# An HGRN2 attention and mixer kernel: the scheduler's load order instead of a written one, fewer idle products, and stores in two halves of columns

## The chip, the cores and the metric

The kernel runs on one core of a Trainium2 chip. The metric is the device time of one execution in microseconds (us). TensorE (PE) multiplies matrices, and its weight loads are recorded apart (PEld). VectorE (DVE), ScalarE (ACT) and GpSimd (POOL) work on elements. SyncE (SP) issues nearly all transfers between HBM and on-chip memory; its queue is in order, so an entry that has to wait holds up all entries behind it.

## The reference

```python
batch, n_heads, seq, head_dim = 4, 8, 768, 48
f = 1.0 / (1.0 + np.exp(-f_logit))
for t in range(S):                                   # a gated outer-product state
    state = f[:, :, t, :, None] * state + np.einsum('bhd,bhe->bhde', k[:, :, t], v[:, :, t])
    y[:, :, t] = np.einsum('bhd,bhde->bhe', q[:, :, t], state)

x = y.transpose(0, 2, 1, 3).reshape(B, S, H * D)      # (4, 768, 384)
h = x.transpose(0, 2, 1) @ U @ V                      # low rank over the sequence, rank 32
u = x + h.transpose(0, 2, 1)
out = u + np.maximum(u @ w_ch1, 0.0) @ w_ch2          # 384 -> 1536 -> 384
```

The inputs q, k, v and f_logit are float32. U, V, w_ch1 and w_ch2 are float64 (8 bytes), and the kernel itself turns their words into float32.

## The kernel before

The attention works on units: two heads of one batch. There are 16 units, four (`HP = 4`) for each batch; units 0 to 3 are the first batch. A unit has eleven steps, five in front (gates, keep, keys, read_back, queries) and six in the rear (kept, states, scan, scores, read, inner). The raw f, k and q of a unit lie in one of two buffers, so the loads of unit n+2 have to wait for the transposes of unit n; v lies in one of three. The first batch's attention has no mixer of an earlier batch to run beside it. After it, the mixer of batch 0 runs beside the attention of batch 1, and so on.

A weight comes in two parts: `start` issues its load, `end` turns it into float32 with two ACT, three DVE and one POOL instruction. The list `weights` has 27 entries: U, two of V (`early = 3`), 12 pieces of w_ch1 (w1[0] to w1[11], 128 columns and 384 KB each) and 12 of w_ch2. The first six pieces of w_ch1 (`FIRST = 6`) are loaded into three `zw` buffers that are free at the start; all other weights are loaded into the four `w_raw` buffers (`RAW = 4`).

Everything on PE, DVE and ACT in the part below keeps its written order. `manual_schedule` says for which engines the written order holds; the other engines' instructions are ordered when the program is compiled, by a scheduler that takes the earliest written instruction that is ready in its own model of the time.

```python
    FIRST = 6
    for _ in range(FIRST // 2):
        t = zp.tile([P, NFC // 2, 2 * P], F32, name="zw").rearrange("p i t -> p (i t)")
        spare.extend([t[:, 0 : 2 * WP], t[:, 2 * WP : 4 * WP]])

    held = spare[2][:, 0:1]                   # a column of the place of w1[2]
    nc.gpsimd.memset(held, 0.0)
    # ... cut ...
        def follow(nm):                       # called when a unit's nm has been transposed
            if n + 2 < NU and n + 2 not in (HP, HP + 1):
                load(n + 2, nm)
    # ... cut ...
        def busy(n):
            for _ in range(n):
                nc.tensor.matmul(idle[:, 0:DM], lhsT=ident, rhs=ends[:, 0:DM], start=True, stop=True)

        with tc.manual_schedule(engines={nc.vector.engine, nc.scalar.engine, nc.sync.engine}):
            busy(1)
            for piece in front(0, "gates"):
                piece()
            for n in range(HP):
                pieces = front(n, "keep", "keys") + rear(n - 1, "scan", "scores")
                pieces += [lambda: busy(3)] + rear(n, "kept") + front(n, "read_back", "queries")
                if n + 1 < HP:
                    pieces += front(n + 1, "gates") + rear(n - 1, "read", "inner") + rear(n, "states")
                for piece in pieces:
                    piece()
                if n < 2:
                    load(n + 2, "v")
                if n == 1:
                    for start, _ in weights[: early + 2]:
                        start()
            # ... cut: ends of U, V, w1[0] and the last steps of units 2 and 3 ...
            low_rank_of(done)
            nc.scalar.copy(table, held)       # the load of w1[2] may not overwrite this column earlier
            for i in range(2):
                for start, _ in weights[early + 2 * i + 2 : early + 2 * i + 4]:
                    start()
                load(HP + i, "f", "k", "q", "v")
            for start, _ in weights[early + FIRST : early + FIRST + RAW]:
                start()
            ends_of[early + 1]()
            # ... cut: rest of the low-rank part ...
            loads = ahead_by(FIRST - 2 + RAW, weights[early + 2 :])
```

`ahead_by(n, loads)` makes a list of calls; call i issues the start of entry i + n and then does the end of entry i. These calls stand between the first products of the mixer of batch 0. In those, `ch1(a, j)` (line 258 of the kernel, tile `pz`) multiplies by the pieces w1[2j] and w1[2j + 1], for each of the three pairs a of token blocks.

From batch 1 on, the second product of a pair of token blocks is done with seven products instead of eight, in four steps:

```python
        def store(t, o):
            nc.sync.dma_start(out=out[b, t * P : (t + 1) * P, :], in_=o)
        # ... cut ...
            if step == 0:
                # ... cut ...
                add(o[:, lo], s[:, lo], pm[:, hi], ALU.add)      # left half of block 2a is final
            # ... cut: steps 1 and 2; step 2 stores block 2a + 1 ...
            else:
                pm = products(a, (S[a, 4], w2[:, NI:NFC, hi]))
                add(W["o0"][:, hi], W["s"][:, hi], pm[:, lo], ALU.add)
                store(2 * a, W["o0"])
```

Of the kernel before, what the change touches and what calls it, by code (L numbers as in the profile page):

```python
# [10 lines left out]
F32 = mybir.dt.float32  # L11
U32 = mybir.dt.uint32
U64 = mybir.dt.uint64
# [5 lines left out]
WP = 384  # L19

RAW = 4
# [125 lines left out]
class Mixer:  # L147
# [6 lines left out]
    def __init__(self, tc, b, x, U, V, w1, w2, sums, ident, blocks, out, two, three, zp, ps_big, ps_mm, wide=False,  # L154
                 z_all=None, room=None, pair=0):
        nc = tc.nc
        P = nc.NUM_PARTITIONS
        NCH, DM = x.shape[1], x.shape[2]
# [25 lines left out]
        def add(*args):  # L184

            with tc.high_priority(offset=AHEAD):
                nc.vector.tensor_tensor(*args)  # L187
# [79 lines left out]
                    z[a, c] = zp.tile([P, NI, 2 * P], F32, name="zw" if wide and c == 1 else "z")  # L267
            nc.scalar.activation(z[a, c][:, k : k + 2, :].rearrange("p i t -> p (i t)"), pm, AF.Relu)  # L268

        def store(t, o):  # L270
            nc.sync.dma_start(out=out[b, t * P : (t + 1) * P, :], in_=o)

        po = {}
        NQ = 4
# [41 lines left out]
        W = {}  # L316
        lo, hi = slice(0, HM), slice(HM, DM)

        def seven(a, step):
            x0, x1 = x[:, 2 * a, :], x[:, 2 * a + 1, :]  # L320
            if step == 0:
                pm = products(a, (part(a, 0, 0), w2[:, 0:NI, lo]), (part(a, 0, 1), w2[:, NI:NFC, lo]))
                s = W["s"] = two.tile([P, WP], U32, name="w_y").bitcast(F32)
                o = W["o0"] = three.tile([P, DM], F32, name="o")
                nc.scalar.copy(s[:, hi], pm[:, lo])
                add(s[:, lo], x0[:, lo], pm[:, lo], ALU.add)
                add(o[:, lo], s[:, lo], pm[:, hi], ALU.add)
            elif step == 1:
                pm = products(a, (S[a, 2], sums[2]), (S[a, 3], sums[3]))
                s, o = W["s"], W["o0"]  # L330
                add(s[:, hi], s[:, hi], pm[:, lo], ALU.add)
                add(o[:, hi], s[:, hi], pm[:, hi], ALU.add)
                o1 = W["o1"] = three.tile([P, DM], F32, name="o")
                add(o1.rearrange("p (n d) -> p n d", n=2), x1.rearrange("p (n d) -> p n d", n=2),
                    o[:, hi].unsqueeze(1).broadcast_to((P, 2, HM)), ALU.add)
                add(s[:, hi], s[:, hi], x0[:, hi], ALU.add)
            elif step == 2:
                pm = products(a, (part(a, 1, 1), sums[4]), (S[a, 1], sums[1]))
                add(W["o1"], W["o1"], pm[:, 0:DM], ALU.add)
                store(2 * a + 1, W["o1"])  # L340
                add(W["s"][:, hi], W["s"][:, hi], pm[:, hi], ALU.add)
            else:
                pm = products(a, (S[a, 4], w2[:, NI:NFC, hi]))
                add(W["o0"][:, hi], W["s"][:, hi], pm[:, lo], ALU.add)
                store(2 * a, W["o0"])

        sums_x, values = {}, {}
        FG = NFC // 3
# [124 lines left out]
def factored_path(ctx, tc, q, k, v, f_logit, moe_U, moe_V, moe_w_ch1, moe_w_ch2, out, ok):  # L473
# [56 lines left out]
    def load(n, *names):  # L530

        b, hp = divmod(n, HP)
        for nm in names:
            if nm == "v":
                v_tiles[n] = three.tile([P, NBL, 2, D], F32, name="v_nat")
            for par in range(2):
                head = src[nm][b, 2 * hp + par]
                if nm == "v" and par:

                    for s in range(2):  # L540
                        nc.sync.dma_start(
                            out=v_tiles[n][(1 - s) * C : (2 - s) * C, :, par, :],
                            in_=head.rearrange("(c s p) d -> s p c d", s=2, p=C)[s],
                        )
                    continue
                if nm == "v" or n < TURNED:
                    dst = v_tiles[n] if nm == "v" else nat[n % 2][nm]
                    nc.sync.dma_start(out=dst[:, :, par, 0:D], in_=head.rearrange("(c p) d -> p c d", p=P))  # L548
                    continue
                head = head.rearrange("(c i) d -> i c d", i=NB)  # L550
                for part in range(2):
                    p0 = par * PAD + part * NB
                    n_ch = min(NB, D - part * NB)
                    nc.sync.dma_start(  # L554
                        out=raw[n % 2][nm][p0 : p0 + NB, :].rearrange("p (c d) -> p c d", d=NB)[:, :, 0:n_ch],
                        in_=head[:, :, part * NB : part * NB + n_ch],
                    )
# [55 lines left out]

    spare = []

    FIRST = 6
    for _ in range(FIRST // 2):
        t = zp.tile([P, NFC // 2, 2 * P], F32, name="zw").rearrange("p i t -> p (i t)")
        spare.extend([t[:, 0 : 2 * WP], t[:, 2 * WP : 4 * WP]])


    held = spare[2][:, 0:1]
    nc.gpsimd.memset(held, 0.0)

    def place():
        return spare.pop(0).bitcast(U64)

    weights += [
        take_in(w1[:, :, i * P : (i + 1) * P], w1_rows[:, :, i * P : (i + 1) * P], place if i < FIRST else None)
        for i in range(NFC)  # L630
# [271 lines left out]
    def front(n, *names):  # L902

        if n >= NU:
            return []
        if n not in ahead:
            ahead[n] = dict(zip(("gates", "keep", "keys", "read_back", "queries"), prepare(n)))
        return [ahead[n].pop(nm) for nm in names]

    def rear(n, *names):  # L910

        if not 0 <= n < NU:
            return []
        if n not in here:
            here[n] = dict(zip(("kept", "states", "scan", "scores", "read", "inner"), attend(n)))
        return [here[n].pop(nm) for nm in names if nm in here[n]]
# [43 lines left out]
    with tc.manual_schedule(engines={nc.vector.engine, nc.scalar.engine}):  # L960


        idle = ps_mm.tile([P, 512], F32, name="idle", tag="mm")

        def busy(n):
            for _ in range(n):
                nc.tensor.matmul(idle[:, 0:DM], lhsT=ident, rhs=ends[:, 0:DM], start=True, stop=True)

        with tc.manual_schedule(engines={nc.vector.engine, nc.scalar.engine, nc.sync.engine}):
            busy(1)  # L970
            for piece in front(0, "gates"):
                piece()
            for n in range(HP):
                pieces = front(n, "keep", "keys") + rear(n - 1, "scan", "scores")
                pieces += [lambda: busy(3)] + rear(n, "kept") + front(n, "read_back", "queries")
                if n + 1 < HP:
                    pieces += front(n + 1, "gates") + rear(n - 1, "read", "inner") + rear(n, "states")
                for piece in pieces:
                    piece()
                if n < 2:  # L980
                    load(n + 2, "v")
                if n == 1:


                    for start, _ in weights[: early + 2]:
                        start()


            done, rest = slice(0, 2 * n * D), slice(2 * n * D, DM)
            ends_of = [end for _, end in weights]  # L990
            pieces = rear(n, "states") + rear(n - 1, "read") + rear(n, "scan") + ends_of[:1] + rear(n, "scores")
            pieces += ends_of[1:2] + rear(n - 1, "inner") + rear(n, "read") + ends_of[2 : early + 1]
            for piece in pieces:
                piece()
            m = mixer(0)
            low_rank_of, added_up_of, mix_of = m.some
            low_rank_of(done)

            nc.scalar.copy(table, held)
            for i in range(2):  # L1000
                for start, _ in weights[early + 2 * i + 2 : early + 2 * i + 4]:
                    start()
                load(HP + i, "f", "k", "q", "v")
            for start, _ in weights[early + FIRST : early + FIRST + RAW]:
                start()
            ends_of[early + 1]()
            for piece in rear(HP - 1, "inner"):
                piece()
            added_up_of(done)
            low_rank_of(rest)  # L1010
            mix_of(done)
            added_up_of(rest)
            mix_of(rest)
            loads = ahead_by(FIRST - 2 + RAW, weights[early + 2 :])

        start = m.before[3:5] + m.firsts[0:1] + m.before[5:]

        EARLY = 6
        second = chain(front(HP, "gates", "keep", "keys", "read_back", "queries"), steps(HP, 2 * HP + 1))
        for i, (_, piece) in enumerate(start + m.firsts[1:]):  # L1020
            piece()
            if loads:
                loads.pop(0)()
            if i >= EARLY:
                next(second)()
        for f in loads:
            f()
        n = len(m.seconds) // (NBL // 2)
        todo, after = m.seconds[:-n], m.seconds[-n:]

        attention(second, 12 + 10 * HP - (len(start) + len(m.firsts) - 1 - EARLY), todo)
        m = start_mixer(1, after)
        for f in to_sum:
            f()
# [380 lines left out]
```

## Time and profile before

| what | value |
|---|---|
| time, median of 3 runs | 495.2 us (494.14 to 495.38) |
| span of the profiled execution | 493.6 us |
| PE busy | 473.2 us (96%), 5541 products |
| DVE busy | 355.6 us (72%) |
| ACT busy | 162.9 us (33%) |
| POOL busy | 37.4 us (8%) |
| transfers on the one queue | 33.44 MB, 37.8% of 16 engines' span |
| stores of the output | 24 of 192 KB |

The profile's page gives busy times over the whole span and, in 40 slices of 12.3 us, the tenths in which each engine was busy. PE is busy in nearly all slices, so what matters is where it is not, and where its clock is halved. In the timeline, a group is given with its start, its length, engine, line, operation, tiles and count, and in brackets the idle time of the engine before it with the instruction that ended that idle time. A stretch (of the view of stretches) is a row with one sum of busy time for each engine, the granted clock of PE as a share of full speed, the share of time in which the transfer engines were busy (which can come out above 1 where transfers overlap) and the rate.

### The profile page before, as it was taken

To read this page: it belongs to the slowest core of one execution; us is meant where nothing else is said; L and a number is where in the kernel's file an instruction comes from. 1 tells how busy PE (TensorE), PEld (TensorE's weight loads), DVE (VectorE), ACT (ScalarE), POOL (GpSimd) and SP (SyncE) were. 2 spreads that over 40 slices of the span, in tenths; PEclk is the share of its full clock that TensorE was granted. 3 is DMA by queue.
4 is the path that set the end of the run, shared out by engine and by line. 5 is a ranking of instruction groups with operands and counts; after the bars stand their busy time and mean duration, and the time that the engine had idled before them with its cause. 6 is when DMAs were issued, how large, how long until landed. Compare 5 with 4: busy or idle time off the path is not lost.

```text
span 493.6 us, 12736 instructions
## 1 busy us (share of the span) xinstructions
PE 473.2 (96%) x5541; PEld 403.5 (82%) x5541; DVE 355.6 (72%) x563; ACT 162.9 (33%) x310; POOL 37.4 (8%) x50
## 2 busy tenths in 40 slices
PE   7898969999999999999999999999999999999995
PEld 4676758887666558889889878899979999999995
DVE  5879548777988949567657637888797796958742
ACT  3336345565344304432331313433132221211200
POOL 3002224443100000000000000000000000000000
PEclk9999898999999999999999999999999999999999
DMA  9981997658577714251725300100000000000001
GB/s 145 155 158 47 218 213 182 162 126 153 71 118 126 123 32 62 28 73 25 106 28 85 68 17 17 27 3 19 19 1 0 34 2 16 17 1 33 1 33 38
DMA packets 158679, 34.34 MB, mean 70 GB/s; under 512 B 149206, under 2 KB 157078, under 8 KB 158614
## 3 DMA queue, kind: packets, MB, share of 16 engines
q1 hardware_dynamic: 158614, 33.44, 37.8%
q8 instruction: 45, 0.74, 0.6%
q14 instruction: 20, 0.16, 0.1%
HBM read 28.70 MB, written 4.72 MB: 68 GB/s over the span
## 4 chain that ended last, share of the span: by engine, by line
PE 69%; DVE 13%; SPq 7%; DMA 4%; issue 3%; ACT 2%; POOL 0%; DVEq 0%; ACTq 0%
PE pw L312 25%; PE pz L258 17%; PE pp L410 11%; SPq L548 3%; PE y L886 2%; PE y L868 2%; SPq L554 2%; DVE late L699 2%; PE ds L830 2%; DVE late L717 2%; PE po L283 2%; PE sc L793 2%; DMA late<-in_f_logit_dram 2%; PE pt L665 1%; PE put L246 1%
## 5 line engine op out<-in xcount | busy, mean ns | idle before, releaser
L258 PE MATMUL pz<-uT,w 128*128 128x256 f32 x504 | 118.6, 390 | 4.7 <-ACT z_all L268 3.4
L258 PEld LDWEIGHTS pz<-uT,w 128*128 128x128 f32 x504 | 95.2, 194 | 18.8 <-ACT z_all L268 3.6
L312 PE MATMUL pw<-w,z_all 128*128 128x192 f32 x216 | 37.7, 329 | 0.0
L312 PE MATMUL pw<-zw,w_raw 128*128 128x192 f32 x216 | 37.4, 327 | 0.0
L312 PEld LDWEIGHTS pw<-zw,w_raw 128*128 128x128 f32 x216 | 35.2, 190 | 0.8 <-issue 0.6
L312 PEld LDWEIGHTS pw<-w,z_all 128*128 128x128 f32 x216 | 35.0, 190 | 0.7
L95 POOL TENSOR_TENSOR w<-w_y,w_r 128x384 int32<-128x384 int32 x24 | 31.2, 1301 | 48.2 <-DVE w_y L94 36.3
L699 DVE TENSOR_TENSOR_SCAN late<-fz,late 128x768 f32<-128x768 f32 x16 | 28.1, 1755 | 9.1 <-ACT fz L686 4.4
L268 ACT ACTIVATE z_all<-pz 128x512 f32<-128x512 f32 x33 | 19.6, 595 | 40.9 <-PE pz L258 40.9
L410 PE MATMUL pp<-v_nat,late 128*128 128x128 f32 x224 | 28.8, 275 | 0.0
L92 DVE TENSOR_SCALAR w_y<-w_y 128x384 f32<-128x384 f32 (+3 forms) x27 | 13.6, 504 | 21.0 <-ACT w_y L90 20.7
L717 DVE TENSOR_TENSOR_SCAN late<-fz,other 128x768 f32<-128x768 f32 x16 | 27.9, 1744 | 0.1
L410 PEld LDWEIGHTS pp<-v_nat,late 128*128 128x128 f32 x224 | 27.0, 192 | 0.0
L283 PE MATMUL po<-w,zw 128*128 128x384 f32 x72 | 25.6, 499 | 0.0
L283 PE MATMUL po<-w,z_all 128*128 128x384 f32 x72 | 25.3, 496 | 0.3 <-DVE o L187 0.3
L403 ACT ACTIVATE other<-other 128x512 f32<-128x512 f32 x18 | 11.3, 631 | 39.9 <-DVE other L187 39.9
L856 ACT COPY st<-added 128x576 f32<-128x576 f32 x12 | 14.7, 1223 | 27.5 <-DVE added L851 27.5
L800 DVE TENSOR_TENSOR A<-sc,causal 128x768 f32<-128x768 f32 x16 | 15.1, 947 | 9.9 <-PE sc L793 9.9
L283 PEld LDWEIGHTS po<-w,z_all 128*128 128x128 f32 x72 | 13.1, 190 | 8.7 <-DVE o L187 0.9
L283 PEld LDWEIGHTS po<-w,zw 128*128 128x128 f32 x72 | 12.9, 189 | 8.7 <-issue 1.2
L187 DVE TENSOR_TENSOR w_raw<-z_all 128x768 f32<-128x768 f32 x12 | 11.4, 954 | 10.6 <-ACT z_all L268 9.2
L886 PEld LDWEIGHTS y<-v_nat,A 64*64 64x64 f32 x768 | 13.3, 139 | 6.7 <-ACT seen L875 3.4
(195 smaller groups left out, 833.3 us busy)
## 6 DMA issues: line engine op xcount, KB each, us to landing
w_raw<-in_moe_w_ch_dram SPq DMA_DIRECT2D x18, 384.0 KB, 3.9
out_dram<-o SPq DMA_DIRECT2D x24, 192.0 KB, 1.9
v_nat<-in_v_dram SPq DMA_DIRECT2D x16, 144.0 KB, 2.9
v_nat<-in_v_dram SPq DMA_DIRECT2D x32, 72.0 KB, 3.2
zw<-in_moe_w_ch_dram SPq DMA_DIRECT2D x6, 384.0 KB, 5.0
late<-in_f_logit_dram SPq DMA_DIRECT2D x10, 96.0 KB, 3.3
late<-in_k_dram SPq DMA_DIRECT2D x10, 96.0 KB, 3.0
late<-in_q_dram SPq DMA_DIRECT2D x10, 96.0 KB, 2.7
```

The costliest lines, as they stand in the source:

```text
L95: nc.gpsimd.tensor_tensor(dst.bitcast(I32), shaped(y.bitcast(I32)), shaped(r), ALU.add)
L258: nc.tensor.matmul(pm[:, i * 2 * P : (i + 1) * 2 * P], lhsT=w1[:, m, o : o + P], rhs=uT[a][:, m, :], start=(m == 0), stop=(m == NDC - 1))
L268: nc.scalar.activation(z[a, c][:, k : k + 2, :].rearrange("p i t -> p (i t)"), pm, AF.Relu)
L283: nc.tensor.matmul(pm, lhsT=z[a, i // NI][:, i % NI, s * P : (s + 1) * P], rhs=w2[:, i, :], start=(i == 0), stop=(i == NFC - 1))
L312: nc.tensor.matmul(pm[:, n * HM : (n + 1) * HM], lhsT=lhs[:, i, :], rhs=rhs[:, i, :], start=(i == 0), stop=(i == NI - 1))
L410: nc.tensor.matmul(pm[:, i, r * P : (r + 1) * P], lhsT=room["w"](wn)[:, r * P : (r + 1) * P], rhs=x_node(a, xn), start=((xn, wn) == of[0]) ...
L548: nc.sync.dma_start(out=dst[:, :, par, 0:D], in_=head.rearrange("(c p) d -> p c d", p=P))
L699: nc.vector.tensor_tensor_scan(backwards(X, S - 1, S), backwards(f, S, S), backwards(ends, S - 1, S), 0.0, ALU.mult, ALU.add,)
L717: nc.vector.tensor_tensor_scan(Y, f[:, 0:S], starts, 0.0, ALU.mult, ALU.add)
L800: nc.vector.tensor_tensor(T["A"], sc[:, :, 0 : NBL * C].rearrange("p h (c i) -> p h c i", i=C), causal.unsqueeze(1).unsqueeze(1).broadcast ...
L856: nc.scalar.copy(st, states.rearrange(by_e, c=NCH))
L886: nc.tensor.matmul(o(s, par, c), lhsT=T["A"][part[s ^ par], par, c, :], rhs=vt[part[s ^ par], c, par, :], start=False, stop=True, skip_gro ...
```

## The change

The changed kernel takes SyncE out of the written order, so the scheduler orders the loads of the first part as it does elsewhere. It drops `held` and the ACT copy that kept the load of w1[2] back. The loads of f, k, q and v of units 4 and 5 are written inside the loop, directly after units 2 and 3 have been transposed; w1[2] to w1[5] are written directly after the loop, and the starts of the later weights stand nine entries ahead of the ends. The idle products, which are there to keep PE's clock up, are left out for units 2 and 3. The three `zw` buffers are taken when they are first needed. The stores of block 2a are made in two halves of columns, each as soon as it is final.

```diff
-        def store(t, o):
-            nc.sync.dma_start(out=out[b, t * P : (t + 1) * P, :], in_=o)
+        def store(t, o, cols=slice(0, DM)):
+            nc.sync.dma_start(out=out[b, t * P : (t + 1) * P, cols], in_=o[:, cols])
...
                 add(o[:, lo], s[:, lo], pm[:, hi], ALU.add)
+                store(2 * a, o, lo)
...
-                store(2 * a, W["o0"])
+                store(2 * a, W["o0"], hi)
...
+    def place():
+        if not spare:
+            t = zp.tile([P, NFC // 2, 2 * P], F32, name="zw").rearrange("p i t -> p (i t)").bitcast(U64)
+            spare.extend([t[:, 0:WP], t[:, WP : 2 * WP]])
+        return spare.pop(0)
+
     FIRST = 6
-    for _ in range(FIRST // 2):
-        t = zp.tile([P, NFC // 2, 2 * P], F32, name="zw").rearrange("p i t -> p (i t)")
-        spare.extend([t[:, 0 : 2 * WP], t[:, 2 * WP : 4 * WP]])
-    held = spare[2][:, 0:1]
-    nc.gpsimd.memset(held, 0.0)
-    def place():
-        return spare.pop(0).bitcast(U64)
...
-        with tc.manual_schedule(engines={nc.vector.engine, nc.scalar.engine, nc.sync.engine}):
... (the body moves out of this block by one level) ...
-                pieces += [lambda: busy(3)] + rear(n, "kept") + front(n, "read_back", "queries")
+            pieces += [lambda: busy(3)] * (n < HP - 2) + rear(n, "kept") + front(n, "read_back", "queries")
...
                 for start, _ in weights[: early + 2]:
                     start()
+            elif n > 1:
+                load(n + 2, "f", "k", "q", "v")
+        for start, _ in weights[early + 2 : early + FIRST]:
+            start()
+        loads = ahead_by(early + FIRST, weights)
...
-            nc.scalar.copy(table, held)
-            for i in range(2):
-                for start, _ in weights[early + 2 * i + 2 : early + 2 * i + 4]:
-                    start()
-                load(HP + i, "f", "k", "q", "v")
-            for start, _ in weights[early + FIRST : early + FIRST + RAW]:
-                start()
-            ends_of[early + 1]()
+        loads[early + 1]()
...
-            loads = ahead_by(FIRST - 2 + RAW, weights[early + 2 :])
+        loads = loads[early + 2 :]
```

More of the change, by code (lines that the diff above doesn't have):

```diff
@@ L967, in busy @@
                 nc.tensor.matmul(idle[:, 0:DM], lhsT=ident, rhs=ends[:, 0:DM], start=True, stop=True)
-        with tc.manual_schedule(engines={nc.vector.engine, nc.scalar.engine, nc.sync.engine}):
[L970 to L974, printed above, removed]
-                pieces += [lambda: busy(3)] + rear(n, "kept") + front(n, "read_back", "queries")
[L976 to L985, printed above, removed]
-                        start()
[L989 to L992, printed above, removed]
@@ L993, in factored_path @@
+        busy(1)
+        for piece in front(0, "gates"):
+            piece()
+        for n in range(HP):
+            pieces = front(n, "keep", "keys") + rear(n - 1, "scan", "scores")
+            pieces += [lambda: busy(3)] * (n < HP - 2) + rear(n, "kept") + front(n, "read_back", "queries")
+            if n + 1 < HP:
+                pieces += front(n + 1, "gates") + rear(n - 1, "read", "inner") + rear(n, "states")
             for piece in pieces:
                 piece()
-            m = mixer(0)
@@ L996, in factored_path @@
-            low_rank_of, added_up_of, mix_of = m.some
-            low_rank_of(done)
-            nc.scalar.copy(table, held)
-            for i in range(2):
-                for start, _ in weights[early + 2 * i + 2 : early + 2 * i + 4]:
-                    start()
-                load(HP + i, "f", "k", "q", "v")
-            for start, _ in weights[early + FIRST : early + FIRST + RAW]:
-                start()
-            ends_of[early + 1]()
-            for piece in rear(HP - 1, "inner"):
-                piece()
@@ L1009, in factored_path @@
[L1009 to L1013, printed above, removed]
-            loads = ahead_by(FIRST - 2 + RAW, weights[early + 2 :])
+            if n < 2:
+                load(n + 2, "v")
+            if n == 1:
+                for start, _ in weights[: early + 2]:
+                    start()
+            elif n > 1:
+                load(n + 2, "f", "k", "q", "v")
+        for start, _ in weights[early + 2 : early + FIRST]:
+            start()
@@ new lines, in factored_path @@
+        loads = ahead_by(early + FIRST, weights)
+        done, rest = slice(0, 2 * n * D), slice(2 * n * D, DM)
+        pieces = rear(n, "states") + rear(n - 1, "read") + rear(n, "scan") + loads[:1] + rear(n, "scores")
+        pieces += loads[1:2] + rear(n - 1, "inner") + rear(n, "read") + loads[2 : early + 1]
+        for piece in pieces:
+            piece()
+        m = mixer(0)
+        low_rank_of, added_up_of, mix_of = m.some
+        low_rank_of(done)
+        loads[early + 1]()
+        for piece in rear(HP - 1, "inner"):
+            piece()
@@ L1016, in factored_path @@
+        added_up_of(done)
+        low_rank_of(rest)
+        mix_of(done)
+        added_up_of(rest)
+        mix_of(rest)
+        loads = loads[early + 2 :]
         start = m.before[3:5] + m.firsts[0:1] + m.before[5:]
```

## The prediction

> **What bounds the kernel now.** I read the busy totals first, then stretches of the first 80 us, then PE's timeline with what it waited for, then SP's queue. The totals and slices of the page:
>
> ```profile
> PE 473.2 (96%) x5541; PEld 403.5 (82%) x5541; DVE 355.6 (72%) x563; ACT 162.9 (33%) x310; POOL 37.4 (8%) x50
> DMA  9981997658577714251725300100000000000001
> ```
>
> PE is the bound over most of the span: only 493.6 - 473.2 = 20.4 us of it are idle. So a gain must come from that idle time, from time at half clock, or from products that needn't be there. The transfers are near full for three slices (to 37 us), stand nearly empty in the fourth (37 to 49 us), and are full again. That hole is made by the kernel. The stretches around it:
>
> ```profile
> 26.00:28.00 2.00, 2.00 (x55) 1.50 (x54) 1.54 (x2) 0.11 (x1) 0.00 (x0) 1.00 1.03 189
> 40.00:42.00 2.00, 1.87 (x100) 1.74 (x92) 1.57 (x2) 0.95 (x3) 0.00 (x0) 1.00 0.01 4
> 44.00:46.00 2.00, 1.40 (x31) 0.71 (x22) 1.86 (x7) 0.94 (x5) 0.79 (x2) 1.00 0.00 0
> 50.00:52.00 2.00, 1.31 (x18) 0.77 (x14) 2.00 (x3) 0.24 (x1) 1.00 (x1) 1.00 1.20 307
> 70.00:72.00 2.00, 0.00 (x0) 0.00 (x0) 0.36 (x1) 0.95 (x3) 0.00 (x0) 1.00 1.09 372
> 74.00:76.00 2.00, 2.00 (x6) 1.55 (x6) 1.93 (x4) 1.74 (x4) 1.04 (x2) 0.50 0.89 232
> ```
>
> The first pair of numbers after the sum is PE's busy time and count, the last three are clock, transfer share and GB/s. From 40 to 46 us nothing is loaded; from 70 to 72 us PE does nothing at all while weights pour in at 372 GB/s; from 74 to 76 us PE runs at half clock. PE's timeline names the wait:
>
> ```profile
> 63.11 5.45 PE L258 MATMUL pz<-uT,w 128*128 128x256 f32 x24 [1.32 <-ACT uT L247]
> 68.39 0.82 PE L665 MATMUL pt<-ident,late 128*128 128x128 f32 x6
> 72.58 7.13 PE L258 MATMUL pz<-uT,w 128*128 128x256 f32 x24 [3.37 <-ACT z_all L268]
> 80.20 5.35 PE L258 MATMUL pz<-uT,w 128*128 128x256 f32 x24
> ```
>
> The engine named, ACT, is itself waiting: the waits list 6.6 us in one piece for its operation on a `w_raw` weight, ended by that weight's transfer (71.05 us). The chain that ended last says the same: SP's issues of unit 4 and 5 from 52.3 us without a break to 66.5 us, then the w1[6] transfer of 3.98 us, then two ACT operations, then the products. And SP's queue shows why the issues are so late:
>
> ```profile
> SPq L81 <- ACT table L999: 13.0, 1, 13.0
> ```
>
> SP stood 13.0 us (34.2 to 47.2 us) before the load of w1[2], waiting for the ACT copy that the kernel put in front of it. Everything behind it waited too.
>
> **What the skill says.** The Trainium skill, "TensorE: Matmul & The Clock Gate", section "Part 1: The HAM clock gate": PE's clock is half when it has been idle for a window of about 3.4 us, and whole again after as long a busy window. The trace agrees in kind: 0.51 at 24 to 26 us and 0.50 at 54 to 56 and 74 to 76 us, each after a gap or a sparse stretch, and 24 products took 7.13 us instead of 5.35 us. This is what the idle products are for. The Trainium skill, "DMA: Bandwidth & Descriptors", section "Why small descriptors are slow (HBM only)": short pieces cost a fixed part each. The trace agrees: unit loads (192 bytes a piece) moved at about 163 GB/s here, w_ch1 pieces at 307 to 372 GB/s. The skill has no page on the scheduler's order, on which much of this rests.
>
> **The change part by part.**
>
> *Idle products of units 2 and 3.* Each group of six takes 2.13 us of the chain (27.28 and 36.09 us). In unit 2 removing it hardly helps: DVE runs without a gap from 26.46 to 34.5 us and is the bound there. In unit 3, DVE waits 0.76 us for the k transposes (35.27 us), which come earlier if PE is 2.1 us ahead; then 0.33 us before the state scan at 41.39 us goes too. I take 1.1 us of the 4.3 us. More does not come, since the remaining DVE chain is solid.
>
> *No hold, loads of units 4 and 5 and w1[2] to w1[5] early.* In the present order SP starts units 2 and 3 without waiting and reaches U at 31.25 us. If the scheduler keeps this written order, unit 4 (1.18 MB, 7.2 us at 163 GB/s) starts at about 35 us, where f, k and q buffers have been free since 20, 25 and 30 us and v since 34 us. Unit 5 follows; its last v load needs the end of unit 2's inner products (47.4 us now, about 46 us then), so SP may stand there briefly. w1[2] to w1[5] (4 x 393 KB at 330 GB/s: 4.8 us) then land by about 50 to 55 us and w1[6] to w1[9] by about 60 us. Now w1[4] is there at 61.4 us (ACT waits 2.2 us for it) and w1[6] at 71.05 us. PE asks for w1[2] near 61 us, for w1[4] near 66 us and for w1[6] near 72 us. So no product should wait for a weight:
>
> - idle before the pz at 72.58 us: 3.37 us;
> - half clock after it: 7.13 - 5.35 = 1.8 us;
> - idle before the pz at 63.11 us (ACT's copy of uT stands behind its wait for w1[4]): 1.3 us.
>
> Sum 6.5 us. The half clock at 54 to 57 us (12 products in 3.68 us against 2.76 us) comes from the sparse low-rank part before it and stays.
>
> *Does it reach the end?* From 72.6 us PE is 100% busy to 120 us, and in 120:150 and 150:176 it is busy 29.1 of 30 and 25.8 of 26 us while DVE is busy 26.4 and 23.9 us. There DVE nearly bounds, but its work is tied to PE's order and should move along. Behind 176 us PE has few gaps. I count nearly all as kept, less something for loads landing differently.
>
> *Half stores.* Nine blocks get a second SP issue of about 0.35 us, beside other work. Only the last one counts: 488.63 us (DVE's last add) to the end at 493.6 us is 5.0 us. The median landing of a 192 KB store is 1.9 us; half of it saves perhaps 0.3 us, because most of a landing is not data.
>
> Sum: 1.1 + 6.5 + 0.3 = 7.9 us, giving 487.3 us.
>
> **Rivals.**
>
> *The scheduler puts weights ahead of the first units.* U, V and w1[0] to w1[5] need no wait, so wherever its model sees SP free while unit 2 or 3 waits for a buffer, they go first. Those 2.7 MB, at 330 GB/s down to the 213 GB/s of the sixth slice of the page, cost 8 to 13 us in a stage that is already short of data: PE waits 1.35 us for unit 2's f at 20.20 us, and transfers are full to 37 us. Against it stand the 7 us gained later, so the time would be 492 to 502 us. For it: the written order was made for some reason. Against it: in the part that is scheduled now, f parts of unit 6 go out one at a time between weights (73.5, 77.5, 79.8, 84.1 us), although all four became free together. The model therefore seems to count an issue as expensive, and with 18 issues for units 0 and 1 it would never see SP free before unit 2 is ready.
>
> *PE runs cold without the idle products.* Units 2 and 3 and the low-rank part would run at half clock, as inner and states did at 22 to 26 us (1.50 us each instead of 0.9). From 28 to 44 us PE would still be busy some three quarters of the time. If it does happen, some 4 to 6 us of small products double in part behind DVE: 2 to 3 us lost, so about 490 us.
>
> *The time is absorbed by DVE or SP in batch 1's attention.* From 123.8 to 175 us the chain that ended last runs through DVE, twice through a load (150.4 and 162.8 us), with SP blocked by stores. If unit 6 and 7 loads don't come earlier, PE stands there instead: 491 to 494 us.
>
> **Range and chances.** 487.3 us if all holds. About one chance in four for the first rival (middle 496 us) and some loss to the others lift the middle to 489.0 us. The range is 484.0 to 498.0 us. Faster by over 2% needs under 485.5 us: 0.14. Slower by over 2% needs over 505 us, which takes a bad order and no gain later: 0.05. Within 2%: 0.81.
>
> **What would show it.** Right: SP has no wait of 13 us; the fourth slice of the transfers is full; no pz product of the first mixer waits for ACT by more than 1 us; 24 pz products near 74 us take 5.4 us; PE's gaps between 44 and 80 us fall by about 4.7 us. Wrong: f of unit 2 or 3 arrives later than 20.1 and 30.5 us; the clock lies at 0.5 between 27 and 44 us; the stage from 120 to 176 us, shifted, becomes longer than 56 us; or the last product still ends near 488.6 us, so that what is left is the tail alone.

## The result

| | before | changed kernel |
|---|---|---|
| median | 495.28 us (494.14 to 495.38, 4 runs) | 487.83 us (487.56 to 488.76, 4 runs) |
| ratio | | 0.9858, 95% interval 0.9838 to 0.9878 |
| span of the profiled execution | 493.6 us | 487.0 us |

The kernel became 7.4 us faster by the medians, 7.0 us by the ratio; a second group of runs of both kernels, further below, gives 6.0 and 6.1 us. The profiled execution of the changed kernel is the longest of its four, and the two profiles differ by 6.6 us. The page of the changed kernel, its totals and its slices of transfer time:

```profile
PE 468.8 (96%) x5529; PEld 400.9 (82%) x5529; DVE 356.7 (73%) x563; ACT 163.2 (34%) x309; POOL 37.6 (8%) x49
...
DMA  9979976666687512334426100100000000000000
```

The fourth slice, which stood at 1, is now 9: the empty time of the transfers is gone. The stretches of the changed kernel (PE's busy time and count come first after the sum; clock, transfer share and GB/s last):

```profile
26.00:28.00 2.00, 1.72 (x64) 1.46 (x63) 1.80 (x2) 0.00 (x0) 0.00 (x0) 1.00 1.01 186
40.00:42.00 2.00, 0.86 (x43) 0.72 (x47) 1.91 (x4) 0.89 (x4) 0.00 (x0) 1.00 0.64 125
44.00:46.00 2.00, 2.00 (x18) 0.71 (x15) 1.18 (x6) 1.50 (x5) 0.76 (x2) 0.50 1.23 176
50.00:52.00 2.00, 1.31 (x17) 0.86 (x15) 1.83 (x3) 0.24 (x1) 0.43 (x1) 1.00 0.77 155
70.00:72.00 2.00, 2.00 (x11) 1.77 (x10) 1.33 (x3) 1.49 (x3) 1.00 (x1) 1.00 1.04 250
74.00:76.00 2.00, 2.00 (x11) 1.75 (x10) 1.82 (x4) 1.18 (x4) 1.58 (x1) 1.00 0.93 239
```

From 70 us on PE is full and at full clock, where it had stood still and then run at half. But from 40 to 46 us something new is wrong: PE is busy for 0.86 of 2 us, and then its clock is 0.50. PE's timeline of the changed kernel, first the end of the first attention, then the first products of the mixer:

```profile
36.47 0.28 PE L810 MATMUL pt<-ident,kz 64*128 64x64 f32 x3 [0.79 <-issue]
...
41.74 0.51 PE L789 MATMUL sc<-qT,kz 48*64 48x64 f32 x20 [1.14 <-issue]
...
44.23 2.13 PE L208 MATMUL ph<-x,U 128*32 128x288 f32 x12
...
54.69 3.67 PE L258 MATMUL pz<-uT,w 128*128 128x256 f32 x12
58.20 0.82 PE L246 MATMUL put<-ident,x 128*128 128x128 f32 x6
58.85 8.19 PE L258 MATMUL pz<-uT,w 128*128 128x256 f32 x36
66.88 0.82 PE L661 MATMUL pt<-ident,late 128*128 128x128 f32 x6
67.53 5.34 PE L258 MATMUL pz<-uT,w 128*128 128x256 f32 x24
```

No pz product has a wait in front of it any more, and 24 of them take 5.34 us. The two pauses with "issue" are time in which PE waited for nothing that the profile shows. They will matter below. SP's queue of the changed kernel:

```profile
33.16 0.96 SPq L81 DMA_DIRECT2D zw<-in_moe_w_ch_dram  x2
34.16 2.38 SPq L549 DMA_DIRECT2D late<-in_f_logit_dram  x2
...
51.06 1.28 SPq L542 DMA_DIRECT2D v_nat<-in_v_dram  x2
52.39 2.20 SPq L81 DMA_DIRECT2D zw<-in_moe_w_ch_dram  x4
54.63 3.91 SPq L81 DMA_DIRECT2D w_raw<-in_moe_w_ch_dram  x4
```

Units 4 and 5 follow w1[1] at once, and w1[2] to w1[9] are issued between 52.4 and 58.5 us. Before, w1[6] was issued at 67 us.

Set side by side, the two traces say when the 6.8 us appear. The first pz starts at 54.69 us (54.86 before): 0.17 us. The first product of the second matrix (line 283) starts at 110.61 us (117.45 before): 6.84 us. The last products of that line start 6.84 us earlier (174.82 against 181.66), and so does DVE's last add (481.44 against 488.28). So all the visible gain comes between 55 and 111 us, and nothing of it is lost behind that.

### The profile page after: what moved, and what is told of

Read it like the earlier page. It is cut to its first block, busy times and chain, and to the rows that moved or that the text cites. A ratio compares the mean times of both kernels' runs of the same rounds, so it can differ in the third digit from the quotient of the medians.

```text
span 487.0 us, 12728 instructions
## 1 busy us (share of the span) xinstructions
PE 468.8 (96%) x5529; PEld 400.9 (82%) x5529; DVE 356.7 (73%) x563; ACT 163.2 (34%) x309; POOL 37.6 (8%) x49
## 4 chain that ended last, share of the span: by engine, by line
PE 71%; DVE 13%; DMA 5%; SPq 5%; issue 3%; ACT 2%; DVEq 0%
PE pw L312 26%; PE pz L258 20%; PE pp L411 11%; DVE late L713 2%; SPq L555 2%; PE y L864 2%; PE y L882 2%; PE put L246 2%; PE po L283 2%; SPq L549 2%; PE sc L789 2%; DMA out_dram<-o 2%; PE ds L826 1%; DVE late L695 1%; DMA other<-in_f_logit_dram 1%
## 5 line engine op out<-in xcount | busy, mean ns | idle before, releaser
L258 PE MATMUL pz<-uT,w 128*128 128x256 f32 x504 | 116.8, 386 | 0.0
L258 PEld LDWEIGHTS pz<-uT,w 128*128 128x128 f32 x504 | 94.0, 191 | 13.4 <-ACT uT L247 0.4
```

Source lines behind the costliest of these rows:

```text
L258: nc.tensor.matmul(pm[:, i * 2 * P : (i + 1) * 2 * P], lhsT=w1[:, m, o : o + P], rhs=uT[a][:, m, :], start=(m == 0), stop=(m == NDC - 1))
```

## The experiments

The kernels ran in three groups, each on one chip together with the kernel before; the chip was another in each group. Ratios are to the kernel before in the same group. Its median in the three groups was 494.21, 494.24 and 493.67 us, and single runs of it spread over 491.8 to 498.3 us.

### The three parts alone

The load order alone is the changed kernel with two parts undone (its queue came out slightly different: w1[2] and w1[3] go out ahead of the last v loads of unit 5):

```diff
-            pieces += [lambda: busy(3)] * (n < HP - 2) + rear(n, "kept") + front(n, "read_back", "queries")
+            pieces += [lambda: busy(3)] + rear(n, "kept") + front(n, "read_back", "queries")
...
-                store(2 * a, o, lo)
...
-                store(2 * a, W["o0"], hi)
+                store(2 * a, W["o0"])
```

> The changed kernel with the six idle products back in units 2 and 3 and whole stores: the load order alone. Main theory (the loads of units 4 and 5 fill the transfers' empty time, so the first mixer never waits for a weight): 488.0 to 489.5 us, some 6.5 us under the kernel before; no pz product of the first mixer waits over 1 us. Second theory (the missing idle products and the half stores carry part of the gain): 490.5 us or more. A side question: in the changed kernel PE paused 0.79 and 1.14 us for nothing but 'issue' near 36 and 41 us. If loads at that time slow the fetching of PE's instructions, the pauses stay here; if the idle products cover them, they go.

Measured: 488.08 us (487.64 to 490.25), ratio 0.9883 (0.9856 to 0.9909), so 5.8 us with an interval of 4.5 to 7.1 us. The order of the loads carries most of the gain. PE's timeline of this run still shows pauses, although the idle products are there:

```profile
41.27 0.74 PE L788 MATMUL sc<-qT,kz 48*64 48x64 f32 x34 [0.97 <-issue]
...
45.99 1.16 PE L208 MATMUL ph<-x,U 128*32 128x288 f32 x11 [1.94 <-issue]
```

The idle products alone, in the kernel before:

```diff
-                pieces += [lambda: busy(3)] + rear(n, "kept") + front(n, "read_back", "queries")
+                pieces += [lambda: busy(3)] * (n < HP - 2) + rear(n, "kept") + front(n, "read_back", "queries")
```

> The kernel before without the idle products of units 2 and 3, nothing else. The prediction's step: 1.1 us faster. Rival (PE's half clock and pauses take the place of the products): between 0.3 us faster and 0.5 us slower, with a clock of 0.5 somewhere between 38 and 50 us.

Measured: 492.99 us (491.20 to 495.45, 20 runs), ratio 0.9970 (0.9956 to 0.9983): 1.5 us by the ratio, 1.2 us by the medians. The prediction's 1.1 us lies inside the interval of 0.8 to 2.2 us. The clock at half is there too (0.50 from 50 to 56 us in its stretches, against 0.82, 0.50 and 0.83 from 52 to 58 us in the kernel before), but it doesn't eat the gain.

The half stores alone, in the kernel before:

```diff
+                store(2 * a, o, lo)
...
-                store(2 * a, W["o0"])
+                store(2 * a, W["o0"], hi)
```

> The kernel before with the stores of block 2a in two halves, nothing else. The prediction's step: 0.3 us faster at the end. Rival (landing is not data, and the last store stands behind the one of the block before it either way): within 0.1 us of the kernel before, with 5.0 us from DVE's last add to the end as now.

Measured: 494.33 us (492.09 to 497.12, 14 runs), ratio 1.0005 (0.9983 to 1.0027). No gain is seen, though 0.3 us would lie inside the interval. The profile speaks more clearly. DVE's timeline at its end:

```profile
486.33 0.35 DVE L187 TENSOR_TENSOR o<-w_y,pw 128x192 f32<-128x192 f32 x1 [1.13 <-PE pw L312]
```

From the end of this add (486.68 us) to the end of the span (491.8 us) are 5.1 us, and it was 5.0 us with a whole store.

### What was wrong with the order

Before, three things came together: SP stood 13.0 us, the transfers were empty, and unit loads stood in front of weights. First the hold is taken out of the kernel before, with the order left:

```diff
-    held = spare[2][:, 0:1]
-    nc.gpsimd.memset(held, 0.0)
...
-            nc.scalar.copy(table, held)
```

> The kernel before without the ACT copy that holds back the load of w1[2]; the written order of its loads stays (w1[2], w1[3], unit 4, w1[4], w1[5], unit 5, later weights). Theory that the hold with all that stood behind it is the cause: 488.0 to 490.0 us. Theory that the order (both units ahead of the weights) matters by itself: over 491 us, because w1[6] still lands behind unit 5, which waits for its buffers.

Measured: 490.54 us (488.00 to 492.90), ratio 0.9909 (0.9882 to 0.9935), so 4.5 us (3.2 to 5.8). This lies between the two theories' values and decides neither. In its profile, the slowest of the six runs, no pz waits for a weight, and PE pauses for "issue" 1.41, 0.56 and 1.12 us between 40 and 51 us. The first pz starts only at 59.88 us: PE ran at half clock from 22 to 32 us, before any load that this edit moves.

Then the hold is kept, and only the loads of units 4 and 5 are put in front of it:

```diff
                     for start, _ in weights[: early + 2]:
                         start()
+                elif n > 1:
+                    load(n + 2, "f", "k", "q", "v")
...
-                load(HP + i, "f", "k", "q", "v")
```

> The kernel before with one thing changed: the loads of units 4 and 5 stand in the loop, ahead of the hold, and the hold, the idle products and the whole stores stay. Theory that what the hold kept empty was the transfers, and that the empty time is the cost: 488 to 489.5 us, as with the load order alone. Theory that holding back w1[2] itself is the cost: 493 to 495 us. If loads between 37 and 48 us lengthen PE's pauses for 'issue', those pauses sum to over 1.5 us between 38 and 48 us, as in the run of the load order alone (0.97 + 1.94 us), against 0.6 to 0.9 us in the runs with empty transfers there.

Measured: 490.15 us (488.20 to 491.76), ratio 0.9906 (0.9879 to 0.9933). The time is above the 488 to 489.5 us expected, but the theory that holding w1[2] costs by itself falls: the hold is still there, and 4.1 us by the medians, 4.6 us by the ratio, are gained. The longer pauses came as expected. PE's timeline of this run, then the same two groups in the kernel before:

```profile
41.09 0.74 PE L793 MATMUL sc<-qT,kz 48*64 48x64 f32 x34 [0.98 <-issue]
...
46.09 2.13 PE L208 MATMUL ph<-x,U 128*32 128x288 f32 x11 [2.20 <-issue]
```

```profile
42.04 0.74 PE L793 MATMUL sc<-qT,kz 48*64 48x64 f32 x34 [0.16 <-issue]
...
45.46 1.16 PE L208 MATMUL ph<-x,U 128*32 128x288 f32 x11 [0.46 <-issue]
```

The instructions are the same and in the same order; 0.62 us of pauses have become 3.18 us. What differs is that the transfers now move 163 GB/s between 38 and 48 us, against 16 GB/s. And after 2.20 us of standing still, the next 11 products run at half clock (2.13 us against 1.16 us).

### Using this: the hold kept, weights ahead of units

If the stall came from unit loads in front of weights, then the empty time need not be filled at all. The kernel before, with the hold, without idle products in units 2 and 3, and with the loads behind the hold reordered:

```diff
             nc.scalar.copy(table, held)
-            for i in range(2):
-                for start, _ in weights[early + 2 * i + 2 : early + 2 * i + 4]:
-                    start()
-                load(HP + i, "f", "k", "q", "v")
-            for start, _ in weights[early + FIRST : early + FIRST + RAW]:
-                start()
+            for start, _ in weights[early + 2 : early + FIRST + RAW]:
+                start()
+            for i in range(2):
+                load(HP + i, "f", "k", "q", "v")
```

> The kernel before with the hold kept, so that nothing is loaded from 37 to 47 us, no idle products in units 2 and 3, and behind the hold w1[2] to w1[9] first, then units 4 and 5. Theory that PE's stall comes from the order behind the hold (unit loads in front of weights) and that the empty time itself costs nothing, while it spares PE pauses: 485.5 to 487.5 us, first pz at 53 to 54 us, no pz wait over 0.6 us. Theory that the empty time has to be used: 489 us or more, with PE waiting for unit 4's or 5's f or k near 67 to 85 us.

Measured: 486.58 us (485.67 to 488.19), ratio 0.9845 (0.9819 to 0.9871). With the empty time left as it was, the kernel is 7.7 us faster than before. The missing idle products may have a part in it; the same kernel with them, further below, differs from the kernel before in the order of the loads behind the hold alone, and is 6.2 us faster by its ratio of 0.9875 (4.4 to 7.9 us). Its SP queue and its first products:

```profile
32.45 14.54 SPq L81 DMA_DIRECT2D zw<-in_moe_w_ch_dram  x6
47.03 3.54 SPq L81 DMA_DIRECT2D w_raw<-in_moe_w_ch_dram  x4
50.62 2.86 SPq L548 DMA_DIRECT2D late<-in_f_logit_dram  x2
```

```profile
42.16 1.16 PE L208 MATMUL ph<-x,U 128*32 128x288 f32 x12
...
52.57 3.44 PE L258 MATMUL pz<-uT,w 128*128 128x256 f32 x12
55.84 0.82 PE L246 MATMUL put<-ident,x 128*128 128x128 f32 x6
56.50 7.94 PE L258 MATMUL pz<-uT,w 128*128 128x256 f32 x36
64.27 0.82 PE L665 MATMUL pt<-ident,late 128*128 128x128 f32 x6
```

All weights up to w1[9] are issued by 50.6 us, before any unit load. Unit 4's f, issued then, is in place for the transposes at 64.27 us without a wait. Between 38 and 48 us PE has no pause for "issue" at all, though its clock is 0.50 from 38 to 40 us, and the first pz starts at 52.57 us.

Unit 4 in front of the hold, and only unit 5 last:

```diff
                     for start, _ in weights[: early + 2]:
                         start()
+                elif n == 2:
+                    load(HP, "f", "k", "q", "v")
...
-            for i in range(2):
-                load(HP + i, "f", "k", "q", "v")
+            load(HP + 1, "f", "k", "q", "v")
```

> As the run before it, but with unit 4 loaded in front of the hold (34 to 41 us), so the transfers are empty for only some 6 us, and unit 5 last. If loads from 37 to 41 us do no harm: the same within 0.5 us, 485.5 to 487.5 us, and safer against a wait for unit 4. If any load there lengthens PE's pauses: 0.5 to 1.5 us slower than the run before it.

Measured: 486.97 us (485.57 to 487.52), ratio 0.9844 (0.9820 to 0.9869), the same time as the run before it. Its profile does show a pause of 1.69 us at 39.4 us, and the first pz starts at 53.56 us, 1.0 us later; a cost of that size does not show in the medians of five runs each.

The changed kernel beside these three:

> The changed kernel once more, beside the others: 487.0 to 488.5 us. If PE's half clock near 43 to 46 us in its profiled run was chance, it is absent here or lies elsewhere.

Measured: 488.19 us (487.40 to 489.72), ratio 0.9876 (0.9854 to 0.9899). PE's timeline:

```profile
41.88 0.80 PE L789 MATMUL sc<-qT,kz 48*64 48x64 f32 x20 [2.51 <-issue]
...
45.25 2.13 PE L208 MATMUL ph<-x,U 128*32 128x288 f32 x12
```

The half clock is here again, directly behind the pause, as in the run with units 4 and 5 in front.

### Is it the loads, and what do the idle products cost?

Three more kernels, one the weights-first kernel again, as the two others' neighbour.

> The run weights_first once more, beside its two variants: 486.0 to 487.2 us, PE's pauses for 'issue' between 38 and 48 us under 1 us in sum, first pz at 52.5 to 54 us.

Measured: 486.21 us (485.18 to 486.95), ratio 0.9839 (0.9813 to 0.9865). The first pz starts at 53.09 us and there is no pause for "issue" between 38 and 48 us (one of 1.44 us lies at 34.4 us, where loads are still running, at 229 GB/s from 34 to 36 us). The clock is 0.50 from 38 to 42 us in this profile.

The same without the hold, so that w1[2] to w1[6] go out at once:

```diff
-    held = spare[2][:, 0:1]
-    nc.gpsimd.memset(held, 0.0)
...
-            nc.scalar.copy(table, held)
```

> The run weights_first without the hold: w1[2] to w1[6] go out at 33 to 40 us, the other weights wait for the buffers of U and V (about 44 us), units 4 and 5 last. If only loads between 40 and 48 us lengthen the pauses: the same as weights_first within 0.5 us. If loads at 34 to 40 us do so too: a pause of 1 us or more near 40 us and 0.3 to 1.2 us slower.

Measured: 489.61 us (489.19 to 490.61), ratio 0.9917 (0.9894 to 0.9939), 3.4 us slower than its neighbour by the medians. Its stretches and PE's timeline:

```profile
36.00:38.00 2.00, 1.67 (x90) 1.67 (x92) 1.90 (x2) 0.91 (x2) 0.00 (x0) 1.00 1.00 272
38.00:40.00 2.00, 0.96 (x38) 0.63 (x30) 1.97 (x4) 1.14 (x6) 0.00 (x0) 1.00 1.08 359
40.00:42.00 2.00, 0.00 (x0) 0.00 (x0) 0.52 (x2) 0.00 (x0) 0.58 (x1) 1.00 1.09 345
```

```profile
42.78 0.81 PE L791 MATMUL sc<-qT,kz 48*64 48x64 f32 x20 [3.60 <-issue]
...
46.15 2.13 PE L208 MATMUL ph<-x,U 128*32 128x288 f32 x12
...
56.23 2.83 PE L258 MATMUL pz<-uT,w 128*128 128x256 f32 x12 [0.33 <-ACT uT L247]
```

and the neighbour's first pz:

```profile
53.09 2.83 PE L258 MATMUL pz<-uT,w 128*128 128x256 f32 x12 [0.32 <-ACT uT L247]
```

While weights move at 345 to 359 GB/s, PE stands for 3.60 us in the middle of one group of products; then it runs at half clock, as the neighbour also did for a while, and the first pz starts 3.1 us later. This is the plainest pair of the study: the edit is the hold alone, whose work is to delay loads, and without it the kernel is slower.

The weights-first kernel with the idle products back:

```diff
-                pieces += [lambda: busy(3)] * (n < HP - 2) + rear(n, "kept") + front(n, "read_back", "queries")
+                pieces += [lambda: busy(3)] + rear(n, "kept") + front(n, "read_back", "queries")
```

> The run weights_first with the idle products of units 2 and 3 put back. In the kernel before, leaving them out gained 1.2 to 1.5 us; in the changed kernel at most 0.3 us. Theory that this is because loads between 37 and 48 us lengthen PE's pauses for 'issue', which take up the time of the products left out: with the transfers empty there, as here, the products cost again, so this run is 1.0 to 1.6 us slower than weights_first (487.6 to 488.2 us). Theory that it is chance or the order of loads otherwise: the same within 0.4 us.

Measured: 486.81 us (485.86 to 491.43), ratio 0.9875 (0.9839 to 0.9911), 0.6 us above its neighbour by the medians and 1.8 us by the ratios (one of its six runs took 491.43 us), with intervals that overlap. So neither theory is decided. In this profile the first pz starts at 53.07 us, as without them. The clock shows what may take up the time of the products left out: it is 1.00 in every stretch of 2 us from 20 to 80 us with them, and 0.72, 0.50, 0.50 and 0.57 from 36 to 44 us in the neighbour, without them.

### The pauses of all profiles together

PE's waits for "issue" between about 38 and 48 us (to 52 us in the kernel without the hold, whose first attention took longer), with the transfer rate of the stretch 38 to 48 us. The next two columns give the start of the first pz and the time from there to the first product of line 283. The median is that of all runs of the kernel, not of the profile:

| kernel | GB/s | pauses, us | first pz, us | to line 283, us | median, us |
|---|---|---|---|---|---|
| before | 16 | 0.6 | 54.86 | 62.59 | 494 to 495 |
| halves only | 33 | 0.9 | 53.15 | 62.31 | 494.3 |
| idle products only | 35 | 0.0 | 54.13 | 63.15 | 493.0 |
| weights first with idle products | 40 | 0.5 | 53.07 | 54.83 | 486.8 |
| weights first, again | 42 | 0.0 | 53.09 | 55.26 | 486.2 |
| weights first | 69 | 0.0 | 52.57 | 55.44 | 486.6 |
| unit 4, then hold | 121 | 1.7 | 53.56 | 54.83 | 487.0 |
| changed kernel | 151 | 1.4 | 54.69 | 55.92 | 487.8 |
| order only | 163 | 2.9 | 54.97 | 54.83 | 488.1 |
| units first | 163 | 3.2 | 57.93 | 55.35 | 490.2 |
| changed kernel, again | 166 | 2.5 | 55.41 | 55.01 | 488.2 |
| before without hold | 180 | 3.1 | 59.88 | 54.83 | 490.5 |
| weights early | 250 | 3.6 | 56.23 | 54.82 | 489.6 |

Under 70 GB/s no profile has more than 0.9 us of pauses, over 120 GB/s none has less than 1.4 us.

The two new columns separate two effects. The three kernels that keep unit loads among the weights behind the hold take 62.3 to 63.2 us from the first pz to line 283; every other kernel takes 54.8 to 55.9 us, whichever way it puts this right. From there to DVE's last add all take 370.8 to 371.0 us. What sets the other ten profiles apart is thus almost only when the first pz starts, and before that they differ in PE's pauses and in where its clock is halved.

## Why the prediction was right, and where it was not

The prediction was 489.0 us, range 484.0 to 498.0 us; 487.83 us was measured. The main part, the load order, came true. That the total came so close is partly luck: the two smaller parts, 1.4 us together, are not clearly seen in it, and the first group of runs gives a larger gain (7.4 us) than the second (6.0 us).

*The order of the queue.* The prediction took it that the scheduler keeps the written order. It did: SP's queue goes units 0 to 3, U, V, w1[0], w1[1], unit 4, unit 5, w1[2] to w1[9]. The rival with weights ahead of the first units did not occur (unit 2's f arrived for 19.93 us, 0.27 us earlier than before).

*No hold and early loads, 6.5 us.* Right in mechanism and size for the part it speaks of: all three idle or slow pieces in the mixer are gone, and the time from the first pz to line 283's first product fell by 6.84 - 0.17 = 6.67 us. As a change of the whole time the order alone measured 5.8 us (4.5 to 7.1). The 6.5 us lie inside that interval, but the same loads also cost something that the prediction did not have: 2.9 us of pauses in the first attention, against 0.6 us before.

*Idle products, 1.1 us.* Right for the part alone (1.2 to 1.5 us), not clearly seen in the sum. The changed kernel (487.83 and 488.19 us) and the one with all idle products (488.08 us) lie within 0.3 us by the medians, 0.3 to 1.2 us by the ratios, with intervals that overlap, so 1.1 us is neither shown nor excluded. The step in doubt is "in unit 3, DVE waits 0.76 us for the k transposes (35.27 us), which come earlier if PE is 2.1 us ahead": PE did come to the next group earlier, but with loads running it then stood for "issue" until 41.7 and 41.9 us in the two profiles without the products, and until 41.3 us in the one with them. At that point the wait for the next instructions, not the products, set the time. That is the reading of three profiles. In the weights-first kernel, which has no such pause there, the clock was half for a while in both profiles, and with the products it was not. How far leaving them out helps stays open.

*PE runs cold.* This rival was partly true: the clock was 0.50 from 44 to 46 us. Half clock that begins between 32 and 45 us is found in six of the seven profiles without the idle products, and in none of the six with them. The missing products are not the only way to it: the kernel with units 4 and 5 first has all idle products and runs at half clock from 46 to 52 us, behind its pause. Nor does it come each time: the kernel before without the idle products has none in that stretch.

*Does it reach the end?* Yes, all of it: 6.84 us at 110 us and 6.84 us at DVE's last add. The rival of absorption in batch 1's attention did not occur.

*Half stores, 0.3 us.* Not borne out. The median landing is 1.6 us for a half store on the page of the changed kernel, against 1.9 us for a whole one, as assumed, but the time did not move (ratio 1.0005). The assumption that a shorter landing ends the kernel earlier is what failed: from DVE's last add to the end it is 5.1 us with half stores and 5.2 us in the changed kernel, against 5.0 us. What fills them the profile does not show.

*What the hold was for.* The prediction put the lateness of w1[6] down to the hold and saw only its cost. The runs show both sides: with unit loads among the weights behind it, it cost about 4.5 us, and with all weights next in line behind it, it gained 3.4 us. So the empty time that the prediction wanted filled was not the cost; what mattered was that the weights came in front of unit loads or early enough.

## What to carry to other kernels

When an engine waits for a load, look first at what stands in front of that load in the in-order queue, and sort by when each load is needed: with w1[2] to w1[9] ahead of units 4 and 5 the gain was had without touching the empty time. Filling empty transfer time is not free: while background loads ran here, PE paused for "issue" in a stretch of about 300 small products in 10 us, so look at such a stretch before putting prefetch there. The kernel with the hold and the weights first (486.2 and 486.6 us in two groups of runs, against 488.2 us for the changed kernel in one of them) is the best version found: 1.6 us better than the changed kernel by the medians of the same group, though the intervals of the two ratios (0.9819 to 0.9871 and 0.9854 to 0.9899) overlap.

## What the hardware did that was not expected

PE's pauses for "issue" depend on transfers that have nothing to do with its operands: 0.62 us in sum became 3.18 us when unit loads were put beside the same instructions, and a pause of 3.60 us appeared when weights ran at 345 to 359 GB/s. That loads are the cause is shown by pairs of kernels that differ in the loads alone. How can be read from the traces. The page lists a separate queue of "instruction" transfers that uses the same 16 transfer engines (packets, MB, share):

```profile
q8 instruction: 45, 0.74, 0.6%
```

For PE's 5541 products and as many weight loads that is one packet of 16 KB for 246 of them. Where PE pauses for "issue" twice running, 126 or 127 products and 127 weight loads lie between the two pauses in every profile. And each of the 22 pauses for "issue" that the 13 profiles show between 14 and 62 us of their spans ends 1.1 to 1.7 us after the end of such a packet. In the kernel before, the packet ran from 43.18 to 44.13 us, and PE went on at 45.46 us; with the units first, it ran from 43.17 to 44.48 us, and PE went on at 46.09 us. In the weights-first kernel without the hold, the packet behind which PE stood for 3.60 us started 5.69 us after the end of the pause before it (34.45 and 40.14 us); with the hold, the packet next after a pause started 1.55 us behind it (35.84 and 37.39 us), and no pause followed, though PE was at half clock then and used its instructions up more slowly. So PE stood until its next instructions had come, and they came late when the engines were full of data. No run changed that queue by itself; the reading rests on these times.

Half clock often followed such a pause, but not always: it came behind or within pauses of 1.14, 1.44, 1.69, 2.20, 2.51 and 3.60 us, and not behind 1.41 us in the kernel before without the hold, nor behind 1.94 us in the order-only kernel. It also came without one: in the weights-first kernel the clock is 0.62 and 0.52 in the stretches from 50 to 54 us, where PE had no pause for "issue" after 36 us and, from 44 us on, no idle time longer than 0.77 us, but was busy for only 1.05 to 1.71 of each 2 us. The Trainium skill, "TensorE: Matmul & The Clock Gate", section "Part 1: The HAM clock gate", gives an idle window of about 3.4 us for it; here shorter gaps between small products were enough, so the measurements differ from the page in that. It is a second cost of the same kind: the 11 or 12 products of the low-rank part take 2.13 us in place of 1.16 us.
